# MLP after a mixture of experts: gathered rows are added one step ahead of their transposes, and output tiles leave from four double buffers on another queue

## The chip, the cores and the metric

The kernel runs on one core of one Trainium2 chip. The metric is the device time of one execution in microseconds (us), the median of several runs. A profiled execution gives a trace with the start and length of every instruction; its time counts from the first to the last instruction (the span).

The core's engines run their own instruction lists in order and wait for each other by semaphores: PE (matrix multiplications), DVE and ACT (elementwise work), POOL (here the indirect gathers) and SP (which issues plain transfers only). ACT and POOL issue transfers too.

## What is computed

Three stages in a row: an attention without softmax, a mixture of eight experts with two experts for each of 2304 tokens, and an MLP. The change touches only the last one and the way its input is brought together:

```python
def _moe2_ref(x, w_in, w_out) -> np.ndarray:      # x (2304, 512), w_in (512, 2048), w_out (2048, 512)
    h = x @ w_in
    g = h * (1.0 / (1.0 + np.exp(-h)))
    return (g @ w_out).astype(np.float32)
```

Here `x` is the output of the experts: each row is the sum of two expert rows, each with its own weight (`out[mask] += top2_w[mask, k, None] * (h @ w2[e])`).

## The kernel before

Every operand of a large product is split into a high and a low part, and three products (high·high, high·low, low·high) are added up in one accumulator. The experts leave their rows in `y_dram`. The MLP then runs over five blocks of tokens: block 0 has 256 tokens, blocks 1 to 4 have 512 each (`BLOCKS`). `Block` brings the input of one block together in tiles of 128 tokens, in four moves for tile t:

- `fetch` (f): POOL gathers the two expert rows of each token from DRAM into two tiles `yg` (line 993). For block 1 these are tiles of the tag `xg` with three buffers in all.
- `add` (a): DVE weighs and adds the two (one `tensor_scalar`, one `scalar_tensor_tensor`).
- `turn` (t): PE transposes the sum, 4 times 128x128, into an accumulator tile `x2ps`.
- `split` (s): ACT copies it into the high part and DVE subtracts to get the low part (`x2T`).

One block is a loop over steps: 8 steps of two column groups of `w_in` in block 0, 16 steps of one in the others. A step s is `mm3` (PE makes `pg`, two buffers; ACT takes the sigmoid of it into `sg`; DVE multiplies; ACT copies the high part `g` and DVE subtracts for the low part), then what `BESIDE` lists for that step, then `mm4` of step s-2 (PE adds `g` times a piece of `w_out` into `pout`). In block 0, `mm3` also splits a piece of `w_out` (`hwout` on ACT, `lwout` on DVE) that SP has loaded (`rwout`); the later blocks find them in place.

`BESIDE` is the table that says beside which step each move of the next block's tiles stands: its first row is for block 0 (which prepares block 1), its second row for the others. PE, ACT and DVE keep the written order; the transfers of POOL and SP stand in their own lists. So what a list puts ahead of an instruction must be done first. `Block` also loads the token weights and row numbers (`rt`, 2 buffers) on SP.

At a block's end `store_out` copies each accumulator tile of 128 tokens with ACT into a tile `ob` (tag `y`, two buffers) and issues its store to `out` from ACT's list, one after the other; then ACT goes on with the next block's `sg`. All PE, DVE and ACT instructions of this part carry line 44, a helper's, so tiles tell them apart.

Of the kernel before, what the change touches and what calls it, by code (L numbers as in the profile page):

```python
# [8 lines left out]
F32 = mybir.dt.float32  # L9
# [4 lines left out]
AF = mybir.ActivationFunctionType  # L14
# [5 lines left out]
P = 128  # L20
PT = 96
CAP = 640
TOP = 2
# [24 lines left out]
def attention_moe_mlp(  # L48
# [15 lines left out]
    nc = tc.nc  # L64
    pe, act, dve = (InOrder(tc, engine) for engine in (nc.tensor, nc.scalar, nc.vector))
    B, H, S, D = q.shape
    N, DM = out.shape
    E, _, F = w1.shape
# [22 lines left out]
    def psA(name):  # L91
        return psum.tile([P, 2, 512], F32, tag="A", name=name)

    def psB(name):
        return psum.tile([P, 512], F32, tag="B", name=name)
# [15 lines left out]
    mp = ctx.enter_context(tc.tile_pool(name="mp", bufs=2))  # L111
# [72 lines left out]
    def wslot(name, dtype=F32R):  # L184
        return wpool[0].tile([P, 1024], dtype, tag="w", name=name)

    def fetch(src, name, shape, raw=None):
        if raw is None:
            raw = raw_pool[0].tile([P, 1024], F32, tag="raw", name="r" + name, bufs=2)
        nc.sync.dma_start(raw if shape is None else raw.rearrange("p (a b) -> p a b", a=shape), src)  # L190
        return raw
# [15 lines left out]
    def fetch_w1(e):  # L207
        return [(fetch(w1_rows(e, c), f"w1_{e}_{c}", None), f"w1_{e}_{c}") for c in range(KD)]

    def fetch_w2(e):  # L210
        return [(fetch(w2_rows(e, i), f"w2_{e}_{i}", 2), f"w2_{e}_{i}") for i in range(KF // 2)]
# [4 lines left out]
    def passes(ws, xs):  # L216
        (wh, wl), (xh, xl) = ws, xs
        return ((wh, xh), (wh, xl), (wl, xh))
# [103 lines left out]
    with ExitStack() as ph1:  # L322
# [4 lines left out]
        for i in range(2):  # L327
            t = att.tile([P, H, 160], F32, name=f"kvbd{i}")
# [345 lines left out]
        q_of(2, 2)  # L674
        kv_of(3, (1,))
        raw1 += [fetch(w1_rows(0, c), "", None, wslot(f"r1_{c}", F32)) for c in range(KD)]
        raw2 += [fetch(w2_rows(0, i), "", 2, wslot(f"r2_{i}", F32)) for i in range(KF // 2)]
        for n in range(2 * JJ):
# [297 lines left out]
    class Block:  # L976
# [7 lines left out]
        def fetch(self, t):  # L984
            src = y_first if self.i == 0 else y_dram

            if self.i == 1:
                ys = [mp.tile([P, DM], F32, tag="xg", name=f"yg1_{t}_{kk}", bufs=3) for kk in range(TOP)]
            else:
                ys = raw_pool[0].tile([P, TOP, DM], F32, tag="raw", name=f"yg{self.i}_{t}", bufs=2)  # L990
                ys = [ys[:, kk, :] for kk in range(TOP)]
            for kk, y in enumerate(ys):
                nc.gpsimd.indirect_dma_start(  # L993
                    out=y, out_offset=None, in_=src,
                    in_offset=bass.IndirectOffsetOnAxis(
                        ap=self.rt[:, t, kk : kk + 1].bitcast(I32), axis=0
                    ),
                )
            self.rows[t] = ys
# [23 lines left out]
    x2_pool = [None]  # L1023
    raw_pool[0] = ctx.enter_context(tc.tile_pool(name="raw_p", bufs=2, reuse_waits="tile"))
    with ExitStack() as ph2:
# [55 lines left out]
        def h_tiles(e, f, n):  # L1081
            return tuple(
                tp.tile([P, CAP], F32R, tag="h", name=f"h{e}_{f}_{l}", bufs=2 * KF)[:, :n] for l in range(2)
            )
# [8 lines left out]
        for e in range(E):  # L1093
# [9 lines left out]
            s0 = PARTS[parts[0]][0]  # L1103
            h = []
            for f in range(KF):
                t = h_tiles(e, f, CAP - s0)
# [55 lines left out]
    with ExitStack() as ph3:  # L1162
        wcp = ph3.enter_context(tc.tile_pool(name="wcp", bufs=8, reuse_waits="tile"))
        gp = ph3.enter_context(tc.tile_pool(name="gp", bufs=2, reuse_waits="tile"))
        x2_pool[0] = gp
        wou = {}

        def fetch_wout(i):
            raw = mp.tile([P, 1024], F32, tag="xT0", name=f"rwout{i}", bufs=4) if i in (2, 3) else None
            return fetch(wout_dram[i].rearrange("(a p) d -> p a d", p=P), f"wout{i}", 2, raw)  # L1170

        def mm3(i, x, s, fs, raw=None):

            pg = psB(f"pg{i}_{s}")
            w = x[0].shape[2]
            for n, f in enumerate(fs):
                fh, fo = divmod(f, 8)
                k = 0
                for c in range(KD):
                    for wt, xt in passes(win[fh, c], x):  # L1180
                        pe.matmul(
                            pg[:, n * w : (n + 1) * w], wt[:, fo * P : (fo + 1) * P], xt[:, c, :],
                            start=(k == 0), stop=(k == 3 * KD - 1),
                        )
                        k += 1
            sg = gp.tile([P, 512], F32, name="sg")
            if raw:
                if s == 4:
                    wpool[0] = wcp
                hi, lo = wou[s] = wslot(f"hwout{s}"), wslot(f"lwout{s}")  # L1190
                act.activation(hi, raw, AF.Copy)
            act.activation(sg, pg, AF.Sigmoid)
            dve.tensor_mul(sg, pg, sg)
            if raw:
                dve.tensor_sub(lo, raw, hi.bitcast(F32))
            gh, gl = (gp.tile([P, 512], F32R, tag="g", name=f"g{i}_{s}_{l}", bufs=8) for l in range(2))
            act.activation(gh, sg, AF.Copy)
            dve.tensor_sub(gl, sg, gh.bitcast(F32))
            return gh, gl

        def mm4(po, g, w, fs):
            for n, f in enumerate(fs):
                ws = tuple(x[:, (f % 2) * DM : (f % 2 + 1) * DM] for x in wou[f // 2])
                for t in range(w // P):
                    gs = tuple(x[:, n * w + t * P : n * w + (t + 1) * P] for x in g)
                    for k, (gt, wt) in enumerate(passes(gs, ws)):
                        pe.matmul(
                            po[t], gt, wt, start=(f == 0 and k == 0), stop=(f == KFF - 1 and k == 2)
                        )

        def store_out(i, po):
            for t, p in enumerate(po):
                ob = mp.tile([P, DM], F32, tag="y", name=f"ob{i}_{t}", bufs=2)
                act.activation(ob, p, AF.Copy)
                s0 = BLOCKS[i][0] + t * P
                act.dma_start(out[s0 : s0 + P, :], ob)

        BESIDE = (  # L1220
# [3 lines left out]
        )  # L1224

        def beside(i, at, nxt):
            what = {"f": nxt.fetch, "a": nxt.add, "t": nxt.turn, "s": nxt.split} if nxt else {}
            for todo in BESIDE[i > 0].get(at, "").split() if nxt else ():
                what[todo[0]](int(todo[1]))

        raws = [fetch_wout(n) for n in range(4)]
        for i in range(len(BLOCKS)):
            now = x
            w = now.width
            nf = 512 // w
            steps = [range(s * nf, (s + 1) * nf) for s in range(KFF // nf)]
            x = Block(i + 1) if i + 1 < len(BLOCKS) else None
            pos = [psA(f"pout{i}_{n}") for n in range(w // 256)]
            po = [pos[t // 2][:, t % 2, :] for t in range(w // P)]
            g = {}  # L1240
            for s, fs in enumerate(steps):
                g[s] = mm3(i, now.x, s, fs, None if i else raws[s])

                if i == 0 and s in (0, 1, 4, 5):
                    raws.append(fetch_wout(len(raws)))
                beside(i, s, x)
                if s >= LAG:
                    mm4(po, g.pop(s - LAG), w, steps[s - LAG])
            for s in range(len(steps) - LAG, len(steps)):
                if s == len(steps) - 1:  # L1250
                    beside(i, "end", x)
                mm4(po, g.pop(s), w, steps[s])
            store_out(i, po)
# [29 lines left out]
```

## Time and profile before

| | |
|---|---|
| median of three runs | 1058.44 us (1055.13 to 1061.42) |
| the profiled execution | 1060.47 us, with a span of 1058.7 us (1.77 us lie around it) |
| PE busy | 988.8 us, 93% of the span |
| DVE, ACT, POOL busy | 49%, 32%, 28% |
| mean granted clock of PE | 0.969 of full speed |

PE is busy almost throughout, so what counts is where it stands still and where it runs at the lower of its two clock levels (1.2 instead of 2.4 GHz). The views used below are the busy times by stretch, the waits of PE, the chain of work that ended last, and the timelines of single engines.

### The profile page before, as it was taken

How to read it: one execution, taken by the hardware profiler on the slowest of the kernel's cores; microseconds unless marked ns; L12 is line 12 of the kernel's file. 1: busy time of each engine (PE TensorE's matmuls, PEld its weight loads, DVE VectorE, ACT ScalarE, POOL GpSimd, SP SyncE). 2: the span in 40 equal slices, each digit the busy share in tenths (PEclk: the TensorE clock that was granted, in tenths of full speed). 3: DMA queues.
4: the chain of work that ended last, by engine and by line, in shares of the span. 5: the costliest groups of instructions: out<-in, count | busy, mean ns of one | idle time of the engine just before them, and what ended most of it. 6: DMA issues, size and time to landing. Idle time of an engine off the chain costs nothing. (4 is left out here: it accounts for less than half of the span.)

```text
span 1058.7 us, 14062 instructions
## 1 busy us (share of the span) xinstructions
PE 988.8 (93%) x5308; PEld 847.7 (80%) x5308; DVE 522.4 (49%) x1035; ACT 334.5 (32%) x509; POOL 301.5 (28%) x315
## 2 busy tenths in 40 slices
PE   6988499999999999999999967899989998999997
PEld 6977468989889897989888766788878887888886
DVE  2498935766676657666663443232323222333221
ACT  2755125333332323333332332221232222123222
POOL 1355626544545454444520220101010110000000
PEclk8989799999999999999999988899999999999999
DMA  9992244666574847456452632201020120001001
GB/s 228 258 311 81 85 129 145 209 195 198 161 232 121 270 139 226 170 193 200 157 193 75 200 125 70 60 1 40 1 80 1 40 66 15 20 20 40 1 1 40
DMA packets 68327, 126.98 MB, mean 120 GB/s; under 512 B 11552, under 2 KB 28960, under 8 KB 68256
## 3 DMA queue, kind: packets, MB, share of 16 engines
q1 hardware_dynamic: 51520, 86.71, 27.5%
q0 software_dynamic: 6080, 19.93, 6.1%
q10 hardware_dynamic: 10656, 19.40, 4.9%
q8 instruction: 43, 0.70, 0.3%
q14 instruction: 28, 0.23, 0.1%
HBM read 92.94 MB, written 33.07 MB: 119 GB/s over the span
## 5 line engine op out<-in xcount | busy, mean ns | idle before, releaser
L44 PE MATMUL ph<-xT,hw 128*128 128x256 f32 (+1 forms) x960 | 212.5, 312 | 0.3 <-DVE h L44 0.3
L44 PE MATMUL py<-hw,h 128*128 128x512 f32 x608 | 199.9, 400 | 7.6 <-DVE h L44 5.5
L44 PE MATMUL pout<-hwout,g 128*128 128x512 f32 x576 | 197.1, 406 | 0.0
L44 PE MATMUL pg<-x2T,hwin 128*128 128x512 f32 (+1 forms) x640 | 186.0, 376 | 6.1 <-DVE sg L44 6.1
L44 DVE TENSOR_TENSOR sg<-pg,sg 128x512 f32<-128x512 f32 x72 | 49.8, 692 | 242.5 <-ACT sg L44 242.4
L44 PEld LDWEIGHTS ph<-xT,hw 128*128 128x128 f32 x960 | 162.6, 189 | 2.0 <-DVE h L44 0.6
L44 PE MATMUL ph<-xT,lw 128*128 128x256 f32 (+1 forms) x480 | 149.7, 312 | 0.0
L44 PEld LDWEIGHTS py<-hw,h 128*128 128x128 f32 x608 | 114.3, 188 | 35.6 <-DVE h L44 8.1
L44 PEld LDWEIGHTS pg<-x2T,hwin 128*128 128x128 f32 x640 | 117.4, 190 | 30.2 <-DVE sg L44 6.9
L44 PEld LDWEIGHTS pout<-hwout,g 128*128 128x128 f32 x576 | 112.2, 195 | 25.6
L44 PE MATMUL pg<-x2T,lwin 128*128 128x512 f32 (+1 forms) x320 | 120.1, 375 | 0.0
L44 PE MATMUL py<-lw,h 128*128 128x512 f32 x304 | 119.9, 394 | 0.0
L44 PE MATMUL pout<-lwout,g 128*128 128x512 f32 x288 | 115.6, 402 | 0.0
L993 POOL DMA_INDIRECT yg<-y_dram,rt x32 | 31.1, 972 | 296.8 <-PE x2ps L44 227.8
L44 ACT ACTIVATE sg<-pg 128x512 f32<-128x512 f32 x72 | 43.1, 598 | 225.0 <-PE pg L44 223.7
L44 DVE SCALAR_TENSOR_TENSOR h<-ph,h 128x640 fp32r<-128x640 f32 (+1 forms) x64 | 50.5, 789 | 81.9 <-ACT h L44 76.0
L44 PEld LDWEIGHTS ph<-xT,lw 128*128 128x128 f32 x480 | 90.6, 189 | 0.0
L44 ACT ACTIVATE h<-ph 128x640 fp32r<-128x640 f32 (+1 forms) x64 | 43.5, 679 | 144.3 <-PE ph L44 135.6
L1076 POOL TENSOR_TENSOR w<-w,bits 128x256 f32<-128x256 f32 x64 | 47.4, 741 | 143.7 <-DVE w L44 104.6
L198 POOL TENSOR_TENSOR lw<-rw,hw 128x1024 fp32r<-128x1024 f32 x28 | 67.5, 2409 | 16.8 <-ACT hw L44 16.8
L44 DVE TENSOR_TENSOR g<-sg,g 128x512 fp32r<-128x512 f32 x72 | 49.8, 692 | 44.7 <-ACT g L44 44.7
L44 PEld LDWEIGHTS pg<-x2T,lwin 128*128 128x128 f32 x320 | 61.0, 191 | 11.7
(185 smaller groups left out, 1230.0 us busy)
## 6 DMA issues: line engine op xcount, KB each, us to landing
rw<-in_moe_w_dram SPq DMA_DIRECT2D x56, 512.0 KB
y_dram<-y ACTq DMA_DIRECT2D x40, 256.0 KB
f<-in_moe_w_in_dram SPq DMA_DIRECT2D x32, 256.0 KB
f<-in_moe_w_out_dram SPq DMA_DIRECT2D x32, 256.0 KB
k<-in_k_dram SPq DMA_DIRECT2D x16, 288.0 KB
v<-in_v_dram SPq DMA_DIRECT2D x16, 288.0 KB
q<-in_q_dram SPq DMA_DIRECT2D x16, 288.0 KB
x_dram<-xh SPq DMA_DIRECT2D x12, 384.0 KB
```

The costliest lines, as they stand in the source:

```text
L44: return lambda *args, **kwargs: self.tc.keep_in_program_order(op(*args, **kwargs))
L198: low.tensor_sub(lo, raw, hi.bitcast(F32))
L993: nc.gpsimd.indirect_dma_start(out=y, out_offset=None, in_=src, in_offset=bass.IndirectOffsetOnAxis(ap=self.rt[:, t, kk : kk + 1].bitcast( ...
L1076: nc.gpsimd.tensor_add(w, w, bits.bitcast(F32))
```

## The change

It has three parts. In block 1 the odd tiles' gathered rows get two buffers of their own (tag `yg1`) in the pool of the MLP stage. The first row of `BESIDE` is rewritten: `add` of a tile stands one step (or more) ahead of its `turn`. And `store_out` uses four buffers of two tiles each (tag `xT0`, whose earlier users are done), with the stores issued from SP's list.

```diff
             if self.i == 1:
-                ys = [mp.tile([P, DM], F32, tag="xg", name=f"yg1_{t}_{kk}", bufs=3) for kk in range(TOP)]
+                pool, tag, bufs = (x2_pool[0], "yg1", 2) if t % 2 else (mp, "xg", 3)
+                ys = [pool.tile([P, DM], F32, tag=tag, name=f"yg1_{t}_{kk}", bufs=bufs) for kk in range(TOP)]
...
         def store_out(i, po):
-            for t, p in enumerate(po):
-                ob = mp.tile([P, DM], F32, tag="y", name=f"ob{i}_{t}", bufs=2)
-                act.activation(ob, p, AF.Copy)
+            for t in range(0, len(po), 2):
+                ob = mp.tile([P, 2, DM], F32, tag="xT0", name=f"ob{i}_{t}", bufs=4)
                 s0 = BLOCKS[i][0] + t * P
-                act.dma_start(out[s0 : s0 + P, :], ob)
+                for n in range(2):
+                    act.activation(ob[:, n, :], po[t + n], AF.Copy)
+                    nc.sync.dma_start(out[s0 + n * P : s0 + (n + 1) * P, :], ob[:, n, :])
...
         BESIDE = (
-            {0: "f0", 1: "f1", 2: "a0 t0 s0", 3: "a1 t1 s1 f2", 5: "f3 a2 t2 s2", 6: "a3 t3 s3"},
+            {0: "f0", 2: "a0", 3: "t0 s0 f1", 4: "a1", 5: "t1 s1 f2", 6: "a2 f3", 7: "t2 s2 a3", "end": "t3 s3"},
```

DVE's list at steps 2 to 4 of block 0, before (`sg<-pg_2` is the multiplication of step 2, `yg_0` the add of tile 0, `x2T_1<-x2ps_0` the low part of its split):

```order
L44 TENSOR_TENSOR sg<-pg_2_6745,sg 128x512
L44 TENSOR_TENSOR lwout_6772<-rwout_6654,hwout_6771 128x1024
L44 TENSOR_TENSOR g_2_1_6778<-sg,g_2_0_6777 128x512
L44 TENSOR_SCALAR yg_0_0_6699<-yg_0_0_6699,rt_6658 128x512
L44 SCALAR_TENSOR_TENSOR yg_0_1_6700<-yg_0_1_6700,rt_6658,yg_0_0_6699 128x512
L44 TENSOR_TENSOR x2T_1_6789<-x2ps_0_6783,x2T_0_6788 128x4x128
L44 TENSOR_TENSOR sg<-pg_3_6804,sg 128x512
L44 TENSOR_TENSOR lwout_6831<-rwout_6656,hwout_6830 128x1024
L44 TENSOR_TENSOR g_3_1_6837<-sg,g_3_0_6836 128x512
L44 TENSOR_SCALAR yg_1_0_6741<-yg_1_0_6741,rt_6658 128x512
L44 SCALAR_TENSOR_TENSOR yg_1_1_6742<-yg_1_1_6742,rt_6658,yg_1_0_6741 128x512
```

The same place in the change:

```order
L44 TENSOR_TENSOR g_2_1_6774<-sg,g_2_0_6773 128x512
L44 TENSOR_SCALAR yg_0_0_6699<-yg_0_0_6699,rt_6658 128x512
L44 SCALAR_TENSOR_TENSOR yg_0_1_6700<-yg_0_1_6700,rt_6658,yg_0_0_6699 128x512
L44 TENSOR_TENSOR sg<-pg_3_6791,sg 128x512
L44 TENSOR_TENSOR lwout_6818<-rwout_6656,hwout_6817 128x1024
L44 TENSOR_TENSOR g_3_1_6824<-sg,g_3_0_6823 128x512
L44 TENSOR_TENSOR x2T_1_6833<-x2ps_0_6827,x2T_0_6832 128x4x128
L44 TENSOR_TENSOR sg<-pg_4_6852,sg 128x512
L44 TENSOR_TENSOR lwout_6879<-rwout_6697,hwout_6878 128x1024
L44 TENSOR_TENSOR g_4_1_6885<-sg,g_4_0_6884 128x512
L44 TENSOR_SCALAR yg_1_0_6836<-yg_1_0_6836,rt_6658 128x512
L44 SCALAR_TENSOR_TENSOR yg_1_1_6837<-yg_1_1_6837,rt_6658,yg_1_0_6836 128x512
```

The add of tile 0 stays where it was; its split moved behind the work of step 3, and the add of tile 1 from step 3 to step 4.

PE's list at the end of step 2 of block 0, before (the transposes of tile 0 stand between `pg` of step 2 and `mm4` of step 0):

```order
L44 MATMUL pg_2_6745<-x2T_0_6602,hwin_3_5950 128x256
L44 MATMUL pg_2_6745<-x2T_1_6603,hwin_3_5950 128x256
L44 MATMUL pg_2_6745<-x2T_0_6602,lwin_3_5951 128x256
L44 MATMUL x2ps_0_6783<-ident,yg_0_1_6700 128x128 x4
L44 MATMUL pout_0_6660<-hwout_6687,g_0_0_6693 128x512
```

In the change the same transposes stand one step later, behind `pg` of step 3:

```order
L44 MATMUL pg_3_6791<-x2T_0_6602,hwin_3_5950 128x256
L44 MATMUL pg_3_6791<-x2T_1_6603,hwin_3_5950 128x256
L44 MATMUL pg_3_6791<-x2T_0_6602,lwin_3_5951 128x256
L44 MATMUL x2ps_0_6827<-ident,yg_0_1_6700 128x128 x4
L44 MATMUL pout_0_6660<-hwout_6729,g_1_0_6735 128x512
```

So 24 matmuls of `pg` and 12 of `pout` now stand between the end of step 2 and the transposes of tile 0.

ACT's list at the end of block 2, before (`ob` are the copies out of the accumulators, DMA their stores, `sg<-pg_0` is the first work for block 3):

```order
L44 ACTIVATE ob_0_7679<-pout_0_7115 128x512
L44 DMA out_dram<-ob_0_7679 128x512
L44 ACTIVATE ob_1_7682<-pout_0_7115 128x512
L44 DMA out_dram<-ob_1_7682 128x512
L44 ACTIVATE ob_2_7685<-pout_1_7116 128x512
L44 DMA out_dram<-ob_2_7685 128x512
L44 ACTIVATE ob_3_7688<-pout_1_7116 128x512
L44 DMA out_dram<-ob_3_7688 128x512
L44 ACTIVATE sg<-pg_0_7695 128x512
```

The same place in the change:

```order
L44 ACTIVATE x2T_0_7622<-x2ps_2_7652 128x4x128
L44 ACTIVATE x2T_0_7622<-x2ps_3_7657 128x4x128
L44 ACTIVATE ob_0_7678<-pout_0_7114 128x512 x2
L44 ACTIVATE ob_2_7683<-pout_1_7115 128x512 x2
L44 ACTIVATE sg<-pg_0_7692 128x512
```

And SP's list in the change, from the last piece of `w_out` on:

```order
L190 DMA rwout_6940<-wout_dram_80 128x2x512
L969 DMA rt_7688<-rt_dram 128x4x4
L1218 DMA out_dram<-ob_0_7107 128x512 x2
L969 DMA rt_8264<-rt_dram 128x4x4
L1218 DMA out_dram<-ob_0_7678 128x512 x2
L1218 DMA out_dram<-ob_2_7683 128x512 x2
L1218 DMA out_dram<-ob_0_8254 128x512 x2
```

The four stores of a block left ACT's list for SP's, where two loads of `rt` (blocks 3 and 4) stand ahead of the stores of blocks 0 and 1.

## Rows read from the trace of the kernel before

**Rows 1.** The page: the span.

```profile
span 1058.7 us, 14062 instructions
```

**Rows 2.** Busy time by stretch: from:to, length, PE, PEld, DVE, ACT, POOL, clock, DMA.

```profile
616.99:681.31 64.32, 46.75 (x233) 40.37 (x234) 22.13 (x31) 14.59 (x22) 9.09 (x10) 0.84 0.24 72
681.31:772.13 90.82, 90.82 (x402) 73.78 (x401) 29.24 (x44) 23.72 (x40) 5.93 (x7) 1.00 0.07 21
772.13:867.62 95.49, 92.43 (x401) 74.87 (x400) 29.15 (x44) 24.01 (x41) 7.55 (x9) 0.98 0.11 34
867.62:963.10 95.48, 92.47 (x401) 74.90 (x400) 29.15 (x44) 24.04 (x41) 5.47 (x6) 0.98 0.10 31
963.10:1052.36 89.26, 89.26 (x385) 71.95 (x383) 22.15 (x32) 22.28 (x37) 0.00 (x0) 1.00 0.03 12
```

**Rows 3.** Waits of PE from 560 us on: total us, times, longest.

```profile
PE x2ps L44 <- DVE yg L44: 18.4, 5, 4.4
PE pg L44 <- DVE sg L44: 6.1, 2, 3.1
```

**Rows 4.** The chain that ended last: start, length, engine, tile, count.

```profile
617.09 0.61 ACT sg L44
617.72 0.69 DVE sg L44
618.41 0.73 DVE lwout L44
619.46 0.69 DVE g L44
620.57 0.76 DVE yg L44
621.38 0.70 PE x2ps L44 x4
622.08 4.30 PE pout L44 x12
...
642.38 2.77 PE pout L44 x12
645.15 2.88 PE pg L44 x24
...
728.99 0.44 PE x2ps L44 x4
```

**Rows 5.** Gathers: one in POOL's timeline; all 32, median us to landing.

```profile
616.11 1.32 POOL L993 DMA_INDIRECT yg<-y_dram,rt  x1 [0.30 <-issue]
```

```profile
yg<-y_dram,rt POOLq DMA_INDIRECT x32, 3.6
```

**Rows 6.** Loads of 512 KB: issues in SP's timeline, a wait in ACT's.

```profile
587.85 1.45 SPq L190 DMA_DIRECT2D rwin<-win_dram  x2
```

```profile
591.61 1.06 ACT L44 ACTIVATE hwin<-rwin 128x1024 fp32r<-128x1024 f32 x1 [1.43 <-DMA rwin<-win_dram]
```

**Rows 7.** ACT's timeline at the ends of blocks 1 and 3.

```profile
772.60 0.34 ACTq L44 DMA_DIRECT2D out_dram<-ob  x1
776.72 0.60 ACT L44 ACTIVATE ob<-pout 128x512 f32<-128x512 f32 x1 [4.15 <-DMA out_dram<-ob]
...
778.55 0.60 ACT L44 ACTIVATE ob<-pout 128x512 f32<-128x512 f32 x1 [1.23 <-DMA out_dram<-ob]
...
779.56 0.60 ACT L44 ACTIVATE sg<-pg 128x512 f32<-128x512 f32 x1 [0.42 <-ACT ob L44]
...
964.70 0.60 ACT L44 ACTIVATE ob<-pout 128x512 f32<-128x512 f32 x1 [1.13 <-DMA out_dram<-ob]
```

**Rows 8.** ACT's timeline at the end of the program.

```profile
1051.04 0.60 ACT L44 ACTIVATE ob<-pout 128x512 f32<-128x512 f32 x1 [4.78 <-PE pout L44]
...
1055.41 0.34 ACTq L44 DMA_DIRECT2D out_dram<-ob  x1
```

**Rows 9.** Busy time by stretch, the experts.

```profile
180.00:560.00 380.00, 374.55 (x2128) 337.35 (x2127) 255.33 (x491) 127.84 (x169) 181.19 (x180) 1.00 0.59 190
```

**Rows 10.** SP's timeline: the load of block 4's `rt`.

```profile
756.12 0.36 SPq L969 DMA_DIRECT2D rt<-rt_dram  x1
```

## The prediction

> **What bounds the kernel now.** I first cut the last 440 us into blocks, because the change touches nothing ahead of them. PE ends `pg` of step 2 of block 0 at 616.99, and the five stretches after it are the rest of block 0 and blocks 1 to 4 [rows 2]. Block 1 is the measure: PE is busy for all of its 90.82 us at a granted clock of 1.00, that is at 2.4 GHz. Block 4 is alike (89.26 us; it turns no tiles for a successor). Blocks 2 and 3 hold nearly the same matmuls and take 95.49 and 95.48 us, at 0.98. The rest of block 0 takes 64.32 us, in which PE is busy for 46.75, at 0.84. So three stretches lose time, and each shows it twice: idle time and a lower clock.
>
> The waits of PE name the two causes [rows 3]. Five waits of the transposes `x2ps` for DVE's `yg` sum to 18.4 us; four of them, one for each tile of block 1, are 4.4 us long (the fifth is short, for block 0, and is not touched). Two waits of `pg` for DVE's `sg`, 3.1 us at most, fall into blocks 2 and 3.
>
> The chain of work shows the first cause step by step [rows 4]. After `pg` of step 2 the way goes through `sg` on ACT (617.09), then DVE's `sg`, `lwout`, `g`, and only then the add `yg` (ends at 621.33); PE, whose next instruction is the transpose, stands from 616.99 to 621.38. The add waits for nothing of its own: it stands behind three DVE instructions of the same step. After the wait PE is at the lower clock level for a while: the next 12 matmuls of `pout` take 4.30 us, the same twelve later 2.77.
>
> The second cause is in ACT's timeline at the end of block 1 [rows 7]. The third copy `ob` waits 4.15 us for the first store, the fourth 1.23 for the second, as there are only two buffers; block 2's first `sg` starts at 779.56, and PE, with two buffers for `pg`, stops. At the end of block 3, with no gathers around, the same wait is 1.13 us and PE doesn't notice.
>
> **The change part by part.** *Adds ahead of transposes.* The add of tile 0 keeps its place on DVE; PE goes on with `pout` of step 0, `pg` of step 3, and only then transposes. What is left of block 0 after 616.99 is 8 times `pout` at 2.77, 5 times `pg` at 2.88 and 4 transposes at 0.44 [rows 4]: 22.16 + 14.40 + 1.76 = 38.3 us, if nothing waits. Against 64.32 [rows 2] that is **26.0 us less**: 17.6 of idle time (4 x 4.39) and 8.4 at the lower clock.
>
> Does anything wait? I place the new steps from 616.99 with these durations. The transposes then stand at 622.64, 634.38, 646.12 and 652.10. The add of tile 0 ends at 621.33 as now. For tiles 1 and 2 the add again stands behind a step's DVE work; from the end of `pg` to the end of the add is 621.33 - 616.99 = 4.34 us [rows 4], and `pg` of steps 4 and 6 end at 628.73 and 640.47: the adds end at 633.1 and 644.8, 1.3 us ahead of their transposes. The add of tile 3 has the split of tile 2 (0.69, as other 128x512 DVE rows) ahead of it: 646.12 + 5.0 = 651.1, 1.0 us early. So the cover is one `pout` group (2.77 us) less the 1.5 us by which the chain is longer than `pg`; if a step were 1.3 us longer on DVE, the wait would come back at that length.
>
> *Gathers.* Those for tiles 1 and 2 no longer wait for buffers that the adds give back, and all stand on POOL, whose list doesn't wait for PE's steps. The last one needs tile 1's buffer, free after its transpose (634.8); issue 1.0 and landing 3.6 [rows 5] make 639.4, and the add that reads it stands at 649.8. Cost 0, with 10 us of cover.
>
> *Pieces of `w_out`.* The four loads for steps 4 to 7 follow the `lwout` of four steps earlier or less; the tightest, for step 6, is issued after `lwout` of step 4 (about 631.2) and wanted by ACT at 635.4, at the latest at 639.4. From issue to use a load of the same size took 591.61 - 587.85 = 3.76 us [rows 6]. Cost 0; with gathers beside it perhaps twice that, still inside.
>
> *Stores.* With four double buffers a copy waits for a store of two blocks earlier, some 180 us ago: no wait. ACT's four copies follow each other (0.60 each), and `sg` is ready when `pg` of step 0 is, as at the end of block 3 [rows 7]. Blocks 2 and 3 then take what block 1 takes: (95.49 - 90.82) + (95.48 - 90.82) = **9.3 us less**. On SP the stores stand behind two loads of `rt`. The one for block 4 waits until block 2's adds are done; it went out at 756.12 [rows 10], 15 us before block 1's stores. It holds nothing back, and a late store would hold back only a buffer two blocks on.
>
> *The end.* Now the last store is issued at 1055.41, 4.37 us after the first copy starts (1051.04), and the span ends 3.29 us later [rows 8, 1]. In the change the third copy waits only for PE's last matmul (1052.36, [rows 2]): copies at about 1052.5 and 1053.1, the last store at about 1053.8. That is **1.5 us less**, if a store takes as long from SP. No row shows a store to `out` from SP. From issue to the next use, a store there took 776.72 - 772.60 = 4.1 us among gathers, a load from SP 3.76, so I bound the end by 0 and 2 us.
>
> The Trainium skill (DMA: Bandwidth & Descriptors, section "Issuing engines are not separate DMA queues") says that transfers from any engine run on the same 16 DMA engines and interleave, and that another issuer saves only issue time. By that rule the move to SP gives nothing to the transfers themselves, and the 4.15 us wait would stand if the buffers had stayed two; the sum would then be 26.0 us, not 36.8. The trace bears the rule out so far: the same store is waited for 4.15 us beside gathers and 1.13 without, on one queue [rows 7].
>
> The sum is 26.0 + 9.3 + 1.5 = 36.8 us. From the profiled execution's own 1060.47 us (span 1058.7) this leaves 1023.7; from the median of the runs, 1058.44, 2.0 us lower, 1021.6. I predict **1022 us**.
>
> **Rivals.**
> *A: some adds stay late.* The cover is 1.0 to 1.3 us a tile. If a slot on DVE or ACT is longer than now (a late piece of `w_out` blocks ACT's `sg`, a late gather blocks DVE), one or two of the four stalls come back, each at up to 26.0 / 4 = 6.5 us: 1028 to 1035. Against it: neither a load nor a gather is within 4 us of its need.
> *B: the block ends stay.* If the copies wait for something else at a block's end (SP's list, or the stores' traffic slowing the loads and gathers beside them), the 9.3 us are not gained: 1031. For it speaks that store traffic does not shrink; against it, that nothing of a block's end is needed again for 180 us.
> *C: slower, by the clock.* PE would now run some 400 us without a break; a block at 1.00 now lasts some 90 us [rows 2]. If the clock fell to 1.2 GHz late in such a stretch, work there would take twice as long; from 37 us of such work on, the change is no gain, and the 89 us of block 4 alone would give 1022 + 89 = 1111. Against it: over the experts PE is busy for 374.55 of 380 us with a granted clock of 1.00 [rows 9].
> *D: it doesn't do what it says.* New buffers move others in memory, and a first use of `yg1` could wait for the last expert's tiles, so that tile 1 comes late throughout: the waits only change their names, 1055 to 1060. Against it: the gathers need the last expert's rows anyway, and the first one of tile 1 goes out at 616.11 without waiting [rows 5], so that expert's work is over by then.
>
> **How the numbers follow.** The forecast has 0.80; A 0.08, B 0.07, C 0.02, D 0.03. Its own range is 1022 with 3 us for the spread of the runs (1055 to 1061) and 1.5 for the end: about 1017 to 1027. To leave out no more than 2 in 10 on the whole I take in B: 1016 to 1031. A difference of 0.5% (5.3 us) is about what a measurement can tell from none here; forecast, A and B are all faster by more: 0.95; D is the same: 0.03; C slower: 0.02.
>
> **What would show it.** Right: no wait of `x2ps` for `yg` after the short one of block 0; the granted clock 1.00 from block 0 on; blocks 2 and 3 of 90.8 us; 38 us from `pg` of step 2 to the end of block 0; ACT's `ob` never waiting for a store. Wrong: a wait of `x2ps` of 1 us or more, a wait of PE for `hwout` or `g`, `sg` at a block's start later than `pg` of step 1, or a last store that ends more than 4 us after its issue.

## The result, and the profile after

The changed kernel takes 1022.18 us (median of 4 runs, 1018.82 to 1024.52) against 1058.85 us of the kernel before in the same measurement (4 runs): a ratio of 0.9654, with a 95% interval of 0.9613 to 0.9695. The profiled execution takes 1021.36 us with a span of 1019.6, which is 39.1 us less than before [rows 1].

The page of the changed kernel, its span and the line of PE (busy us, share of the span, instructions):

```profile
span 1019.6 us, 14077 instructions
...
PE 976.2 (96%) x5308; PEld 838.9 (82%) x5308; DVE 522.4 (51%) x1035; ACT 333.3 (33%) x509; POOL 301.9 (30%) x315
```

PE's busy time fell by 12.6 us (988.8 to 976.2) with as many instructions: the same matmuls ran less often at the lower clock. The rest of the gain is idle time.

Busy time by stretch of the changed kernel, cut at the same events as [rows 2] (from:to, length, PE, PEld, DVE, ACT, POOL, granted clock, DMA); the last row is what follows PE's last matmul:

```profile
615.06:653.35 38.29, 38.29 (x234) 34.12 (x233) 21.93 (x31) 14.29 (x22) 10.70 (x11) 1.00 0.42 123
653.35:744.21 90.86, 90.86 (x401) 73.76 (x401) 29.24 (x44) 23.92 (x40) 6.08 (x7) 1.00 0.07 21
744.21:835.05 90.84, 90.84 (x401) 73.77 (x401) 29.23 (x44) 23.92 (x40) 7.55 (x9) 1.00 0.12 35
835.05:925.89 90.84, 90.84 (x401) 73.78 (x401) 29.23 (x44) 23.92 (x40) 5.26 (x6) 1.00 0.10 32
925.89:1014.97 89.08, 89.07 (x384) 71.79 (x383) 22.14 (x32) 21.86 (x36) 0.00 (x0) 1.00 0.03 12
1014.97:1019.60 4.63, 0.00 (x0) 0.00 (x0) 0.00 (x0) 1.08 (x2) 0.00 (x0) 0.97 0.61 227
```

Set against [rows 2] this is where the 39.1 us went: 26.0 in the rest of block 0 (64.32 to 38.29), 9.3 in blocks 2 and 3 (95.49 and 95.48 to 90.84 each), 1.7 at the end (1058.7 - 1052.36 = 6.34 to 4.63), 0.1 in blocks 1 and 4, and 1.9 ahead of the change (616.99 to 615.06), where nothing was changed: over the executions shown below that moment lies between 614.67 and 620.74. From 615.06 to its last matmul PE is busy throughout, at a granted clock of 1.00.

All waits of PE from 560 us on in the changed kernel (total us, times, longest), which answer to [rows 3]:

```profile
PE py L44 <- DMA rt<-rt_dram: 2.1, 1, 2.1
PE x2ps L44 <- DVE yg L44: 1.0, 1, 1.0
```

Both lie ahead of the change. The chain of work has no DVE or ACT left in it where [rows 4] had five (start, length, engine, tile, count):

```profile
606.25 8.81 PE pg L44 x72
615.06 2.77 PE pout L44 x12
617.84 2.88 PE pg L44 x24
620.71 0.44 PE x2ps L44 x4
621.15 2.79 PE pout L44 x12
```

Every piece ends where the next begins, and the `pout` group behind the transposes of tile 0 takes 2.79 us instead of 4.30.

ACT's timeline at the end of block 2 in the changed kernel, against [rows 7]:

```profile
833.72 1.09 ACT L44 ACTIVATE ob<-pout 128x512 f32<-128x512 f32 x2 [0.72 <-PE pout L44]
835.09 1.09 ACT L44 ACTIVATE ob<-pout 128x512 f32<-128x512 f32 x2 [0.28 <-PE pout L44]
837.93 0.60 ACT L44 ACTIVATE sg<-pg 128x512 f32<-128x512 f32 x1 [1.76 <-PE pg L44]
```

The four copies wait for PE alone, and are done 1.8 us before the next `sg` has something to read.

### The profile page after: what moved, and what is told of

Read it like the earlier page. It is cut to its first block, busy times and chain, and to the rows that moved or that the text cites. A ratio compares the mean times of both kernels' runs of the same rounds, so it can differ in the third digit from the quotient of the medians.

```text
span 1019.6 us, 14077 instructions
## 1 busy us (share of the span) xinstructions
PE 976.2 (96%) x5308; PEld 838.9 (82%) x5308; DVE 522.4 (51%) x1035; ACT 333.3 (33%) x509; POOL 301.9 (30%) x315
## 5 line engine op out<-in xcount | busy, mean ns | idle before, releaser
L44 PE MATMUL pout<-hwout,g 128*128 128x512 f32 x576 | 191.8, 395 | 0.0
L44 PEld LDWEIGHTS pout<-hwout,g 128*128 128x128 f32 x576 | 108.2, 188 | 24.3
L44 PE MATMUL pout<-lwout,g 128*128 128x512 f32 x288 | 112.9, 392 | 0.0
```

Of the source, the lines that this page charges most:

```text
L44: return lambda *args, **kwargs: self.tc.keep_in_program_order(op(*args, **kwargs))
```

## The experiments

Each was measured against the kernel before on the same chip. From one such group of runs to another the median of the kernel before lies between 1058.85 and 1062.84 us, so a gain is taken within its group. I give for each the median, the ratio with its interval, and the two lengths in which the parts of the change show: "rest of block 0" from the end of `pg` of step 2 to the first `pg` of block 1, and blocks 2 and 3.

### One part at a time: the adds alone, the stores alone

The first takes the new `BESIDE` row and the `yg1` buffers without the new `store_out`, the second the new `store_out` without the other two, each as in the diff of the change.

> Only the new table and the buffers of their own for the odd tiles; the output copies and stores as before. Theory (the parts are independent): the rest of block 0 takes 38.3 us instead of 64.3, blocks 2 and 3 stay at 95.5 us each, the end stays; 26 us less than before, about 1032. Rival (the parts overlap, so that the block ends were partly an effect of block 0's lateness): blocks 2 and 3 change too, and the time is 1022 to 1028, or more than 1036 if block 0 needs the new stores as well.

Measured: 1034.56 us, ratio 0.976 (0.9729 to 0.9791). Block 0's rest takes 38.08 us, blocks 2 and 3 take 95.57 and 95.27.

> Only the four double buffers with the stores on SP's list; adds, transposes and buffers of the gathers as before. Theory: the four waits of the transposes for the adds stay at 4.4 us, blocks 2 and 3 take 90.8 us, the end is 1.7 us shorter; 11 us less than before, about 1048. Rival (the wait moves to something else at the block ends): blocks 2 and 3 stay above 93 us, 1053 to 1058.

Measured: 1049.87 us, ratio 0.9916 (0.9884 to 0.9948). Block 0's rest takes 66.59 us, blocks 2 and 3 take 90.84 each. Busy time by stretch of the first, blocks 2 and 3:

```profile
745.38:840.95 95.57, 92.48 (x402) 74.99 (x401) 29.15 (x44) 24.05 (x41) 7.59 (x9) 0.98 0.11 34
840.95:936.22 95.27, 92.45 (x401) 74.90 (x400) 29.16 (x44) 24.04 (x41) 5.45 (x6) 0.98 0.10 31
```

And of the second, the rest of block 0 and block 2:

```profile
614.80:681.39 66.59, 48.15 (x233) 41.51 (x233) 22.14 (x31) 14.60 (x22) 10.05 (x11) 0.82 0.24 71
...
772.23:863.07 90.84, 90.84 (x401) 73.77 (x400) 29.25 (x44) 23.95 (x40) 7.58 (x9) 1.00 0.11 36
```

Each part moves its own stretch and leaves the other's: the two gains are independent, and they add up. With the adds alone the time is 25.7 us under that of the kernel before in its group (1060.24), with the stores alone 10.4: together 36.1, of which the change shows 36.7.

The 66.59 us of the second kernel are 2.3 more than before, though block 0 is unchanged there. Its add of tile 0 waited 0.91 us for its gather (DVE's timeline); the rest is the work right behind the waits, which ran slower, at a mean granted clock of 0.82 instead of 0.84 for the stretch:

```profile
619.26 0.75 DVE L44 SCALAR_TENSOR_TENSOR yg<-yg,rt,yg 128x512 f32<-128x512 f32 x1 [0.91 <-DMA yg<-y_dram,rt]
```

### Buffers without the queue, the queue without buffers

The third kernel has the four double buffers with the stores still issued by ACT, the fourth the old two buffers with the stores issued by SP (the first pair of lines against the second kernel, the last against the kernel before):

```diff
-                    nc.sync.dma_start(out[s0 + n * P : s0 + (n + 1) * P, :], ob[:, n, :])
+                    act.dma_start(out[s0 + n * P : s0 + (n + 1) * P, :], ob[:, n, :])
...
-                act.dma_start(out[s0 : s0 + P, :], ob)
+                nc.sync.dma_start(out[s0 : s0 + P, :], ob)
```

> The four double buffers, but the stores still issued from ACT's list; the rest as before. Theory (the number of buffers carries the gain, the queue next to nothing): blocks 2 and 3 take 90.8 to 91 us, ACT's copies are about 1.0 us apart and still done before the next block's first sg; 10 us less, about 1049. Rival (the queue carries it): blocks 2 and 3 stay at 95.5, about 1058.

Measured: 1050.52 us, ratio 0.9913 (0.9887 to 0.9938); blocks 2 and 3 take 90.84 each. The buffers alone carry the whole gain at the block ends; what they lack is some of the end (5.64 us after the last matmul instead of 4.63).

> Two single buffers as before, but the stores issued from SP's list; the rest as before. Theory: the third copy still waits for the first store, some 4 us beside the gathers; blocks 2 and 3 stay at 95 to 95.5 us, about 1058. Rival (the queue carries the gain): blocks 2 and 3 at 90.8, about 1048.

Measured: 1053.61 us, ratio 0.9943 (0.992 to 0.9966): a clear gain where my theory expected none. Blocks 2 and 3 take 92.13 and 91.10 us. ACT's timeline at the ends of blocks 1 and 2:

```profile
772.29 1.09 ACT L44 ACTIVATE ob<-pout 128x512 f32<-128x512 f32 x2 [0.72 <-PE pout L44]
777.76 1.22 ACT L44 ACTIVATE ob<-pout 128x512 f32<-128x512 f32 x2 [4.38 <-DMA out_dram<-ob]
...
864.42 1.09 ACT L44 ACTIVATE ob<-pout 128x512 f32<-128x512 f32 x2 [0.72 <-PE pout L44]
869.18 1.09 ACT L44 ACTIVATE ob<-pout 128x512 f32<-128x512 f32 x2 [3.67 <-DMA out_dram<-ob]
```

The third copy waits for a store as before, 4.38 us and 3.67, but the fourth follows without a wait of its own. In the kernel before both waited, 4.15 and 1.23 us at the end of block 1 [rows 7], and at the end of block 2 (ACT's timeline):

```profile
870.71 0.60 ACT L44 ACTIVATE ob<-pout 128x512 f32<-128x512 f32 x1 [2.62 <-DMA out_dram<-ob]
...
874.02 0.60 ACT L44 ACTIVATE ob<-pout 128x512 f32<-128x512 f32 x1 [2.71 <-DMA out_dram<-ob]
```

At the end of block 1 ACT is done 6.7 us after the first copy began instead of the 8.6 of before, and at the two block ends PE waits 1.0 and 0.2 us instead of 3.1 and 3.0.

### What the queue did: spacing or the queue itself

Two buffers, ACT's list, but both copies of a pair stand ahead of both stores:

```diff
-            for t, p in enumerate(po):
-                ob = mp.tile([P, DM], F32, tag="y", name=f"ob{i}_{t}", bufs=2)
-                act.activation(ob, p, AF.Copy)
-                s0 = BLOCKS[i][0] + t * P
-                act.dma_start(out[s0 : s0 + P, :], ob)
+            for t in range(0, len(po), 2):
+                obs = [mp.tile([P, DM], F32, tag="y", name=f"ob{i}_{t + n}", bufs=2) for n in range(2)]
+                for n in range(2):
+                    act.activation(obs[n], po[t + n], AF.Copy)
+                for n in range(2):
+                    s0 = BLOCKS[i][0] + (t + n) * P
+                    act.dma_start(out[s0 : s0 + P, :], obs[n])
```

> The kernel before with its two single buffers and ACT's list, but both copies of a pair ahead of both stores, so that the two stores are issued 0.4 us apart instead of 1.0. It is to tell why the move to SP's list alone, with two buffers, brought blocks 2 and 3 from 95.5 to 92.1 and 91.1 us. Theory (spacing: on SP the second copy doesn't stand behind the first store's issue, so the second store goes out earlier and both land together): blocks 2 and 3 at 92 to 93.5 us, about 1054. Rival (the queue itself: stores from ACT's list land later beside the gathers): blocks 2 and 3 at 95 us or more, 1059 or more.

Measured: 1054.99 us, ratio 0.994 (0.9915 to 0.9965); blocks 2 and 3 take 92.30 and 91.52 us. ACT's timeline at the end of block 1:

```profile
774.94 1.09 ACT L44 ACTIVATE ob<-pout 128x512 f32<-128x512 f32 x2 [0.72 <-PE pout L44]
775.57 0.82 ACTq L44 DMA_DIRECT2D out_dram<-ob  x2
780.08 1.17 ACT L44 ACTIVATE ob<-pout 128x512 f32<-128x512 f32 x2 [4.06 <-DMA out_dram<-ob]
```

This is nearly the fourth kernel's gain without SP. So it is not the queue: in the kernel before, the issue of a store (0.34 us and the handing over around it) stands between two copies, the second store goes out 1.0 us after the first, and its landing, the later one, holds the fourth copy. On SP's list, or with the stores behind both copies, that wait is gone. The chain of work at the end of block 1 goes by the second store in the kernel before, and by the first in the fourth kernel:

```profile
772.60 5.92 DMA out_dram<-ob
778.55 0.61 ACT ob L44
...
772.92 4.74 DMA out_dram<-ob
777.76 0.61 ACT ob L44
```

Why half a microsecond less between the issues does so much is not shown. The second store's buffer was free again 5.9 us after the issue at both block ends before, and here at most 4.6 and 3.8 us after it; the four gathers run beside it in both.

### The gathers beside the stores

The kernel before, with the first four gathers of blocks 2 to 4 held back by one-column copies on POOL into the tiles that they fill (the gathers overwrite them):

```diff
+            if self.i >= 2 and t < 2:
+                for y in ys:
+                    nc.gpsimd.tensor_copy(y[:, :1], g[1][1][:, :1].bitcast(F32))
```

> The kernel before, with the first four gathers of blocks 2 to 4 held back until step 1 of the block before has made its g (four one-column POOL copies into the tiles that they fill, which the gathers overwrite), so that they no longer run beside the stores at a block's end. Stores, buffers and queue as before. Theory (the gathers make the stores slow): the third copy waits 1.1 us for its buffer at every block end, as at the end of block 3, PE doesn't wait, blocks 2 and 3 take 90.9 us; about 9 us less than before, 1050. Rival (two buffers are too few whatever runs beside): blocks 2 and 3 stay above 93 us.

Measured: 1053.07 us, ratio 0.9934 (0.9908 to 0.9959); blocks 2 and 3 take 91.33 and 90.84 us. At the end of block 1 the third copy waits 2.10 us, at the end of block 2 (ACT's timeline):

```profile
865.50 0.34 ACTq L44 DMA_DIRECT2D out_dram<-ob  x1
866.58 0.60 ACT L44 ACTIVATE ob<-pout 128x512 f32<-128x512 f32 x1 [1.12 <-DMA out_dram<-ob]
867.21 0.34 ACTq L44 DMA_DIRECT2D out_dram<-ob  x1
867.59 0.60 ACT L44 ACTIVATE ob<-pout 128x512 f32<-128x512 f32 x1 [0.41 <-DMA out_dram<-ob]
```

At the end of block 2 two buffers suffice once no gathers run beside the stores: the wait is that of block 3's end in [rows 7], and block 3 takes 90.84 us. At the end of block 1 the third copy still waits 2.10 us and block 2 takes 0.5 us too long, though no gather runs there either; that is left open. So nearly all of the old loss needed both, two buffers and four gathers set free at the same moment.

### Block 1's own buffers for the odd tiles

The changed kernel, with all gathers of block 1 back in the three `xg` buffers:

```diff
-                pool, tag, bufs = (x2_pool[0], "yg1", 2) if t % 2 else (mp, "xg", 3)
-                ys = [pool.tile([P, DM], F32, tag=tag, name=f"yg1_{t}_{kk}", bufs=bufs) for kk in range(TOP)]
+                ys = [mp.tile([P, DM], F32, tag="xg", name=f"yg1_{t}_{kk}", bufs=3) for kk in range(TOP)]
```

> The changed kernel, with the gathers of block 1 back in the three buffers of the tag xg. Theory (the table does it, the buffers have slack): the second gather of tile 1 waits for the add of tile 0, lands some 5 us before its own add, and PE doesn't wait; 1022, the rest of block 0 at 38.3 us. Rival (the own buffers are needed): one or two gathers come late, one or two waits of the transposes of 1 us or more, 1025 to 1035.

Measured: 1022.45 us, ratio 0.9623 (0.9595 to 0.9652); the rest of block 0 takes 38.08 us. POOL's timeline shows the second gather of tile 1 waiting, and DVE's the add that reads it:

```profile
625.35 0.94 POOL L993 DMA_INDIRECT yg<-y_dram,rt  x1 [4.18 <-DVE yg L44]
```

```profile
636.06 0.75 DVE L44 SCALAR_TENSOR_TENSOR yg<-yg,rt,yg 128x512 f32<-128x512 f32 x1
```

There are 10.7 us between issue and use, and the add waits for nothing. The own buffers gain nothing here; the table does it.

### The lower clock behind the waits

The kernel before, with matmuls into the accumulator that the transposes overwrite:

```diff
-            self.ps[t] = turn_x(self.rows.pop(t)[1], psC(f"x2ps{self.i}_{t}"))
+            xt_ps = psC(f"x2ps{self.i}_{t}")
+            for _ in range(30 if self.i == 1 else 0):
+                pe.matmul(xt_ps[:, :HA], win[0, 0][0][:, :P], now.x[0][:, 0, :], start=True, stop=True)
+            self.ps[t] = turn_x(self.rows.pop(t)[1], xt_ps)
```

> The kernel before, with 30 matmuls of 256 columns (some 3.5 us, their results are overwritten) ahead of the four transposes of block 1, so that PE works while it waits for the add. Theory (8.4 of the 26 us are the lower clock after the waits): the transposes come no earlier, but the pout groups behind them take 2.8 us instead of 4.0 to 4.75 and the granted clock stays at 1.00; 8 us less than before, about 1050. Rival (the slow groups have another cause, such as traffic or the other engines): they stay slow, about 1058.

Measured: 1053.22 us, ratio 0.992 (0.9887 to 0.9953). The rest of block 0 takes 56.46 us, at a granted clock of 1.00. The chain of work at tile 0:

```profile
619.06 0.66 PE x2ps L44 x4
619.72 2.79 PE pout L44 x12
622.50 2.88 PE pg L44 x24
```

The add comes as late as before (4.39 us after `pg`, now 3.59 of it filled), and the group behind is at 2.79 us. With work in the wait, 7.9 us (64.32 - 56.46) are back: so they were the price of the lower clock behind an empty wait, and not of the add itself.

### A longer chain on DVE

The changed kernel with the subtraction for the low part of `g` done five times in block 0:

```diff
-            dve.tensor_sub(gl, sg, gh.bitcast(F32))
+            for _ in range(5 if i == 0 and s >= 2 else 1):
+                dve.tensor_sub(gl, sg, gh.bitcast(F32))
```

> The changed kernel, with the last DVE instruction of each step of block 0 from step 2 on done five times instead of once (2.4 us more per step, the same result). Theory (the cover of the adds is one pout group less 1.5 us): from the end of pg to the end of the add it takes 6.8 us instead of 4.3, against a step of 5.65; the transposes of tiles 0 to 3 wait some 1.1 us each, in all 4 to 5 us, about 1027, with little or no loss of clock. Rival (something else sets the moment of the adds, such as the gathers): no new wait, 1022. Second rival (waits of this size bring back the whole loss of 6.5 us a tile): 1040 or more.

Measured: 1029.81 us, ratio 0.9712 (0.9671 to 0.9753), 7.4 us above the changed kernel without its `yg1` buffers, which was measured in the same group (1022.45). The rest of block 0 takes 44.95 us, 6.7 more than in the changed kernel. Waits of PE from 606 us on:

```profile
PE x2ps L44 <- DVE yg L44: 6.0, 4, 1.7
```

The repeats took 2.9 us, not 2.4 (3.59 us for five, the first 0.69). From the end of `pg` to the transposes that makes 4.39 + 2.9 = 7.3 us against a step of 5.65: 1.6 us, and the waits are 1.72, 1.66 and 1.68 for tiles 0 to 2, and 0.99 for tile 3. Behind them the clock stays at 1.00 and `pout` at 2.79 us, so waits of this size cost little more than themselves, and the second rival falls.

## Why the prediction was right

**The adds.** The step "26.0 us less" measured 26.0 in the change and in the kernel with the adds alone (64.32 to 38.08, 26.2). Its split held too: 17.6 of idle time and 8.4 at the lower clock were forecast, and filling the waits gave back 7.9.

**The cover.** For tiles 1 to 3 the estimate (the pout group less 1.5 us) stands. In the changed kernel their adds end 1.3, 1.3 and 1.0 us ahead of their transposes, as forecast; for tile 1 (DVE's timeline, then the chain of work):

```profile
630.40 0.75 DVE L44 SCALAR_TENSOR_TENSOR yg<-yg,rt,yg 128x512 f32<-128x512 f32 x1
...
632.46 0.44 PE x2ps L44 x4
```

And a DVE chain longer by 2.9 us brings waits of the size that follows from it. For tile 0 it was off: I put its add at 621.33 "as now", 1.3 us early, and left its gather out. In the changed kernel that add waited for the second gather (DVE's timeline):

```profile
618.13 0.55 DVE L44 TENSOR_SCALAR yg<-yg,rt 128x512 f32<-128x512 f32 x1
619.65 0.75 DVE L44 SCALAR_TENSOR_TENSOR yg<-yg,rt,yg 128x512 f32<-128x512 f32 x1 [0.96 <-DMA yg<-y_dram,rt]
```

It ended at 620.40, 0.3 us before the transposes at 620.71. The kernel before had the same gather in time in its profiled execution; in four of the six other kernels with the old table it was 0.6 to 0.9 us late. So rival A was nearer than I priced it, and that tile 0 brought back no wait hung on 0.3 us. "Neither a load nor a gather is within 4 us of its need" holds for the gathers of tiles 1 to 3 only. The load of `w_out` for step 6 went out at 629.43 and ACT read it at 634.93: with the 3.76 us of [rows 6] that is, as an estimate, 1.7 us early. The sentence that the gathers for tiles 1 and 2 no longer wait for what the adds give back was wrong for the second one of tile 2, at no cost, as its add stands at 641.64 (POOL's timeline):

```profile
620.67 0.94 POOL L994 DMA_INDIRECT yg<-y_dram,rt  x1 [0.99 <-DVE yg L44]
```

**The stores.** "9.3 us less" measured 9.3. The reason given, the number of buffers, is enough by itself (blocks of 90.84 us with ACT's list). But the sentence that with two buffers on SP the wait "would stand", and the gain be nothing, failed: with two buffers, SP's list alone gave 3.4 and 4.4 us, 7.7 of the 9.3 (95.49 to 92.13, 95.48 to 91.10). The 4.15 us wait did stand, as 4.38; the one behind it, for the second store, went, and with it most of PE's wait. I had priced the block's end by the first store's wait, where the chain goes by the second's. By the rule of the Trainium skill (DMA: Bandwidth & Descriptors, "Issuing engines are not separate DMA queues") the queue saves no more than the time to initiate the transfers. The runs agree: with the stores issued from ACT behind both copies nearly the same is gained. What I had not weighed is that in ACT's list that time (0.34 us) stands between two copies.

**The end.** 1.5 us forecast, 1.7 measured, in two parts: 0.7 by the buffers (6.34 to 5.64), 1.0 by SP's list (5.64 to 4.63). The 4.1 us that I took for a store among gathers (776.72 - 772.60) paired the second store's issue with the first one's buffer. The first was issued at 771.59 (ACT's timeline of the kernel before), so it took 5.1 us, and the second 5.95; the bound of 0 to 2 us on the end rests on that figure, the 1.5 does not.

```profile
771.59 0.34 ACTq L44 DMA_DIRECT2D out_dram<-ob  x1
```

**The rivals.** B and D fell with PE's waits: none is left from block 0's step 2 on. C fell too: the granted clock is 1.00 over five stretches of 400 us in all. The median of the runs, 1022.18, agrees with 1022 more closely than the runs' own spread (1018.82 to 1024.52) allows one to claim.

## What to carry to other kernels

When an engine waits at the place where a step's work is both made and used, put a step of its own work between making and using; the cover is the length of that work less the growth of the chain, and it can be read from two rows before it is built. Price such a wait with the lower clock behind it: here four waits of 4.39 us cost 26.0, 6.5 each. And before giving a store more buffers, look at what runs beside it and at what stands between the copies: each of three edits (more buffers, stores behind the copies, gathers some 10 us later) took most of the same 9.3 us away.

## What the runs showed of the hardware

PE's clock: in the kernel before, after each wait of 4.39 us with nothing in it, the next 12 matmuls of `pout` took 4.03 to 4.75 us instead of 2.77, in a stretch whose mean granted clock lay between the 1.2 and the 2.4 GHz level (0.84 [rows 2]). After its wait of 3.06 us in block 2 the next 12 of `pg` took 4.35 us instead of 2.80. After waits of 0.8 us behind filling matmuls and of 0.99 to 1.72 us, no group of `pout` was slower than 2.79. A store of 256 KB to DRAM, issued at 772.60 beside four gathers, held its buffer until 778.55 [rows 7], 5.95 us; without gathers (the kernel that holds them back), one issued at 865.50 gave its buffer back by 867.59, 2.1 us. And the DVE subtraction repeated into one tile (the kernel with the longer chain) took 0.72 us a time, where differing ones follow each other at 0.60 to 0.61.
